# Attention outputs kept as features for the output projection, with maxima turned by VectorE, in a fp32 adaLN block on one Trainium2 core

## The chip, the cores and the metric

The kernel runs on one NeuronCore of a Trainium2 chip. A core has TensorE (PE: matmuls and transposes, with its weight loads as PEld), VectorE (DVE), ScalarE (ACT), GpSimd (POOL) and SyncE (SP), each with an instruction stream of its own, and 16 DMA engines, which are fed from queues; SP's and GpSimd's are used here. A matmul leaves its result in a PSUM bank; every bank holds 128 x 512 numbers of fp32, and in attention the scores, maxima, outputs and small transposes take their banks in turn.

The metric is the device time in microseconds (us), as a median over runs of the whole program.

## The reference

One transformer block with adaptive layer norm, on 2048 rows (S) of 576 features (D), with 32 heads of 18 features (DH) and 4608 hidden features (F):

```python
mod = (_silu(c) @ w_mod).reshape(c.shape[0], 6, 1, -1)
sa, ca, ga, sb, cb, gb = (mod[:, 0], ..., mod[:, 5])
h = _layernorm(x) * (1 + ca) + sa
q, k, v = heads of (h @ wqkv)                 # 32 heads, Dh = 18
p = softmax(q @ k.T * Dh ** -0.5)
x = x + ga * ((p @ v as (S, D)) @ wo)
h = _layernorm(x) * (1 + cb) + sb
x = x + gb * ((sigmoid(h @ w_gate) * (h @ w_up)) @ w_down)
```

All of it is fp32. The kernel gets there with pairs: a number is split into a part `hi` that the matmul format fp32r holds exactly, and the rest `lo`, and a product is made of hi x hi, hi x lo and lo x hi.

## The kernel before

**Stages.** The modulation, the first layer norm and the projections of q, k and v take 236 us; q and k go to DRAM (`qd`, `kd`) as features x rows, in two parts. Attention runs from 236 to 1597 us. The gated part with its products (L1028) and the way down (L1064) takes the rest, to 2927 us.

**Attention's units and steps.** Attention has 32 units. Unit u has a pair of heads, p = u mod 16, and one half of the queries (1024 of them; half 0 in units 0 to 15, half 1 in units 16 to 31). Each unit has 16 steps, kt = 0 to 15, one for 128 keys. What a step does stands in a string of letters, one for odd and one for even steps, which fixes PE's order by hand (the scheduler puts PE's instructions as they are written; it sorts those of the other engines itself):

- `t` is one score matmul (L927), keys x queries, followed by the exponential on ScalarE (L931). Four in a step.
- `v` is `values()`: the exponentials of two steps ago times the values (L548). The accumulator has four groups of 32 partitions, one for each head and half of the unit's queries: 18 features and, in row 18 (DH), the sum of the exponentials. All 16 steps add up in one bank.
- `m` is `turn()`, one step of the generator `maxima()` for a later unit: a matmul queries x keys (L446), of which VectorE takes the maximum over 512 keys (L452). In the units called paired, ScalarE puts one bank in four into SBUF (`over`, L455) and VectorE takes the maximum of that and of another bank in one instruction (L457). The table `SINGLE` names the units that aren't paired. The last of a unit's maxima comes seven steps before the unit starts, at kt 9 of the unit before it; the negated maxima `nm` (L464) have queries on partitions, 128 x 16.
- `k` is `taken()`: at kt 1 the finished accumulator of the unit before is copied by ScalarE into `oT` (L562), which has one buffer. ScalarE does its work in order: the exponentials behind the copy wait until `oT` is free.
- `w`, in odd steps, takes one step of whatever else is under way.

**What hangs on `w` before the change.** At kt 3 `outputs()` turns `oT` with four PE transposes (L572) so that queries lie on partitions, VectorE takes the reciprocals of the sums from PSUM (L576), ScalarE copies the bank back to `oT` (L587), and GpSimd multiplies by the reciprocals (L591) into `Oa` (half 0) or `big` (half 1), row layout. Eight steps of `m` after a unit's maxima are through, `spread()` turns `nm` with one PE transpose (L477), ScalarE and VectorE split it into two parts (L480, L481) and SP writes four rows (L485) into the unit's `q` tile: the score matmul gets the maximum as two more rows of its contraction. In steps 240 to 436 `w` also advances `first_rows()`: `load_wo()`, then `project_o(t)` for the row tiles t = 0 to 7 (output projection: transposes of `Oa`, L652 and L669, a split on VectorE and GpSimd, 28 matmuls L685, the residual), the second layer norm's statistics, and the tiles' transposition and splitting into operands, on GpSimd for the most part. From then on it advances `last_rows_project()`, tiles 8 to 15 over the first 384 features; the other 192 go through DRAM (`oend`) and are done by `last_rows()` amid the gated part, with transposes of its own (L1124, L1131).

**Loads.** `load_heads(u + 2)` stands at the start of unit u: eight SP transfers for the q tile (one of three) and the k tile (one of three) of the unit after next. In steps 64 to 239 GpSimd also prepares the weights of the way down (`down_parts`), with transfers on its own queue.

## Time and profile before

| | us |
|---|---|
| median of 3 runs | 2933.69 |
| the three runs | 2927.91, 2933.69, 2934.46 |
| profiled execution, its own time | 2929.86 |
| profiled execution, span | 2927.5 |

The granted clock of TensorE is 0.995 over the span. The span runs from the first to the last instruction; the execution's own time has a little around it.

How to read the rows in the prediction. The busy line names each engine, its busy time, its share of the span and its instructions. A row of single instructions has the start in us, the duration, the engine, the line of the kernel, the operation, the output and inputs with their shapes, and in brackets how long the engine had been idle and what ended that. A grouped row has the line, engine, operation, output<-inputs, shapes and count, then the busy time and the mean in ns of one, then the idle time in front of the group's instructions and what ended it. Rows with "x6: 616/617/618, 492.0 to 692.1" give a count, the smallest, median and largest duration in ns, and the start of the first and the last one.

### The profile page before, as it was taken

What the parts mean: (1) busy time and instruction counts of PE and PEld (TensorE: products, weight loads), DVE (VectorE), ACT (ScalarE), POOL (GpSimd) and SP (SyncE); (2) the same over time, 40 slices, a digit from 0 to 9 for tenths busy, and PEclk for the clock granted to TensorE, in tenths of its full rate; (3) what the DMA queues carried; (4) which work ended last, traced back from release to release, by engine and by line L of the source; (5) the groups of instructions that cost most, each with busy time, mean ns of one, the idle gap of its engine ahead of it and who ended that gap; (6) DMA issues with size and microseconds to landing.
All of it is one profiled execution on the core that took longest, in us unless ns stands there. A gap on an engine that the chain in (4) does not pass through costs nothing.

```text
span 2927.5 us, 46356 instructions
## 1 busy us (share of the span) xinstructions
PE 2848.3 (97%) x17141; PEld 1879.6 (64%) x17141; DVE 2218.6 (76%) x4023; ACT 1581.4 (54%) x2955; POOL 649.4 (22%) x829
## 2 busy tenths in 40 slices
PE   7999999999999999999999899999999999999998
PEld 6964333333444444444443788877888888888888
DVE  7277888888899988999982878789777555555555
ACT  3216889999987778998788333333332111111111
POOL 3122014544213110761102222233221100000000
PEclk9999999999999999999999999999999999999999
DMA  5344124333212110222125866677556844554443
GB/s 180 120 157 128 52 76 140 133 120 123 84 56 76 35 56 23 101 98 66 52 87 177 284 216 234 231 277 247 207 201 233 301 170 167 167 168 167 159 159 136
DMA packets 136745, 429.25 MB, mean 147 GB/s; under 512 B 18884, under 2 KB 56520, under 8 KB 124232
## 3 DMA queue, kind: packets, MB, share of 16 engines
q1 hardware_dynamic: 120472, 344.99, 35.0%
q0 software_dynamic: 16048, 81.31, 7.9%
q8 instruction: 135, 2.21, 0.3%
q14 instruction: 90, 0.74, 0.1%
HBM read 267.77 MB, written 157.95 MB: 145 GB/s over the span
## 4 chain that ended last, share of the span: by engine, by line
PE 82%; DVE 7%; ACT 4%; DMA 3%; issue 3%; SPq 1%; POOL 0%; POOLq 0%; ACTq 0%; DVEq 0%
PE o L548 16%; PE d L1064 14%; PE x L1028 12%; PE s L446 11%; PE s L927 10%; PE bu L1028 4%; PE bg L1028 4%; PE s L274 4%; ACT p L931 3%; PE s L325 2%; PE s L685 2%; DVE mx L452 1%; DVE w L1020 1%; DMA B<-hs 1%; PE s L572 1%
## 5 line engine op out<-in xcount | busy, mean ns | idle before, releaser
L452 DVE TENSOR_REDUCE mx<-s 128x1 f32<-128x512 f32 x1696 | 1076.6, 684 | 126.3 <-PE s L446 108.3
L931 ACT ACTIVATE p<-s 128x512 f32<-128x512 f32 x2048 | 1068.4, 610 | 146.7 <-PE s L446 75.2
L446 PE MATMUL s<-k,q 54*128 54x512 f32 x1920 | 608.4, 451 | 12.2 <-ACT p L931 6.6
L548 PE MATMUL o<-p,vaug 128*32 128x512 f32 x4096 | 554.8, 607 | 0.5 <-ACT p L931 0.4
L927 PE MATMUL s<-q,k 56*128 56x512 f32 x1920 | 552.6, 425 | 1.3 <-DMA q<-mrows 0.8
L1064 PE MATMUL d<-wd,hh 128*128 128x288 f32 x2304 | 468.3, 297 | 20.8 <-DVE Oa L1068 20.2
L927 PEld LDWEIGHTS s<-q,k 56*128 56x128 f32 x1920 | 260.5, 186 | 295.2 <-DVE mx L452 184.7
L446 PEld LDWEIGHTS s<-k,q 54*128 54x128 f32 x1920 | 273.6, 184 | 250.3 <-ACT p L931 172.3
L1064 PEld LDWEIGHTS d<-wd,hh 128*128 128x128 f32 x2304 | 373.4, 188 | 35.6 <-DVE Oa L1068 26.4
L1068 DVE TENSOR_TENSOR Oa<-Oa,d 128x288 f32<-128x288 f32 x576 | 256.0, 452 | 125.5 <-PE d L1064 120.3
L1064 PE MATMUL d<-wd,hl 128*128 128x288 f32 x1152 | 340.7, 296 | 0.0
L1028 PE MATMUL x<-k,w 128*128 128x512 f32 x1008 | 242.4, 390 | 4.7 <-DVE u L1239 2.4
L1040 ACT ACTIVATE u<-u 128x512 f32<-128x512 f32 x72 | 45.5, 632 | 318.3 <-DVE u L1228 312.1
L1064 PEld LDWEIGHTS d<-wd,hl 128*128 128x128 f32 x1152 | 216.9, 188 | 0.0
L1028 PEld LDWEIGHTS x<-k,w 128*128 128x128 f32 x1008 | 186.7, 188 | 42.5 <-DVE u L1239 3.5
L548 PEld LDWEIGHTS o<-p,vaug 128*32 128x32 f32 x4096 | 83.4, 108 | 163.9 <-issue 151.4
L1037 ACT ACTIVATE sg<-x 128x512 f32<-128x512 f32 x36 | 21.5, 599 | 304.3 <-PE x L1028 304.3
L1070 POOL DMA_DIRECT2D out_dram<-Oa x16 | 8.7, 543 | 606.0 <-DVE Oa L1068 606.0
L455 ACT ACTIVATE over<-s 128x512 f32<-128x512 f32 x176 | 105.1, 597 | 33.5 <-PE s L446 28.4
L1028 PE MATMUL x<-big,w 128*128 128x512 f32 x504 | 120.6, 390 | 1.0 <-issue 1.0
L1028 PE MATMUL x<-w,w 128*128 128x512 f32 x504 | 121.0, 390 | 0.0
L457 DVE CUSTOM_DVE_ANT_0 over<-s,over 128x512 f32<-128x512 f32 x176 | 120.2, 683 | 0.3
(232 smaller groups left out, 3605.1 us busy)
## 6 DMA issues: line engine op xcount, KB each, us to landing
ws<-w SPq DMA_DIRECT2D x126, 640.0 KB
w<-ws SPq DMA_DIRECT2D x126, 640.0 KB
wd<-wds SPq DMA_DIRECT2D x36, 1152.0 KB
k<-kd SPq DMA_DIRECT2D x60, 360.0 KB
wds<-w POOLq DMA_DIRECT2D x18, 1152.0 KB, 4.5
k<-kd SPq DMA_DIRECT2D x60, 180.0 KB
w<-in_B_w_down_dram POOLq DMA_DIRECT2D x18, 576.0 KB, 4.3
q<-qd SPq DMA_DIRECT2D x64, 144.0 KB
```

Source lines behind the costliest of these rows:

```text
L274: nc.tensor.matmul(acc, w, hT[:, t, cols], start=n == 0, stop=n == len(ts_) - 1)
L325: nc.tensor.matmul(acc[:, 0:HALF], hT[:, k, rows], w, start=n == 0, stop=n == len(ts_) - 1,)
L446: nc.tensor.matmul(sp, qs[rows, qt * P : (qt + 1) * P], ks[rows, at * 512 : (at + 1) * 512], start=True, stop=True,)
L452: nc.vector.tensor_reduce(to, sp, axis=AX.X, op=ALU.max)
L455: nc.scalar.activation(over, sp, AF.Relu)
L457: nc.vector.tensor_tensor_reduce(out=over, in0=sp, in1=over, scale=1.0, scalar=LOWEST, op0=ALU.add, op1=ALU.max, accum_out=mx[:, h * n + q ...
L548: nc.tensor.matmul(acc[32 * j : 32 * j + 32, :], vaug[:, kt, (2 * p + h) * VW : (2 * p + h) * VW + 32], probs[2 * c + h], start=kt == 0, s ...
L927: nc.tensor.matmul(sT, ks[rows, kcols], qs[rows, c * 512 : (c + 1) * 512], start=True, stop=True)
L931: state["exp"] = nc.scalar.activation(pr, sT, AF.Exp, scale=SCALE)
L1028: nc.tensor.matmul(acc[v], w[:, v, a, :], X[s][:, b, :], start=first and n == 0, stop=n == 6, skip_group_check=not first,)
L1064: nc.tensor.matmul(acc[:, :HALF], a[:, f, rows], w[:, f, cols], start=n == 0, stop=n == 5)
L1068: nc.vector.tensor_add(Oa[:, t, cols], Oa[:, t, cols], acc[:, :HALF])
```

## The change

**Outputs.** `taken()` now asks `outputs()` for a list of seven entries, one for each following `w`: at kt 1, right behind the copy, SP gathers the four rows of sums of `oT` into `sums`, 128 x 16; in the next `w` VectorE takes their reciprocals, SP writes these to DRAM and reads them back, each row spread over 32 partitions, into `full`, 128 x 512. Three `w` later GpSimd multiplies `oT` by `full`, and makes the two parts; two later SP stores both parts to the DRAM tile `od`, features x queries. No transposes by PE, no copy back on ScalarE. `full` and the parts lie in `Oa` (units of half 0), `big` (half 1) or a temporary (unit 30's outputs), in three places used in turn, and for the last unit in tiles of the exponentials.

**Maxima.** `nm` gets 128 x 32 with zeros behind the 16 columns. VectorE turns it in blocks of 32 x 32 (L466), makes the two parts (L468, L469) at once, and SP writes them to DRAM (`rows_m`) and reads four rows from there into the `q` tile. `spread()` is gone.

**Projection.** `project_o` reads its operands ready from `od`, one tile ahead, by SP; its transposes, copies and splits are gone, its matmuls stay. `last_rows()` reads the 192 features from `od` as well; its 16 transposes and the splits are gone, and so is `oend`. `last_rows` starts at n >= 11 instead of 5.

**Order.** The order by hand now holds for VectorE and SP too, and not for PE alone. `load_heads(u + 2)` stands behind step kt = 1 of unit u, and thus behind the gather. `SINGLE` has units 19 and 20 no more, so that they are paired. `FROM1` is eight steps later, and `load_wo` takes four more steps.

On SP, between unit 7 and unit 8, `q` being the tile of queries, `k` that of keys, and `mrows` the rows of maxima, this stood before:

```order
L485 DMA q_981<-mrows 1x8x128 x4
L411 DMA q_983<-qd 36x1x1024
L414 DMA q_983<-qd 18x1024
L415 DMA k_2181<-kd 36x1x2560
L419 DMA k_2181<-kd 18x2560
...
L485 DMA q_982<-mrows 1x8x128 x4
```

and this stands there now, `sums` and `rec` being the sums and reciprocals, `Oa` the place of `full` and of the parts:

```order
L571 DMA sums<-oT 128x1x16
L413 DMA q_983<-qd 36x1x1024
L416 DMA q_983<-qd 18x1024
L417 DMA k_2190<-kd 36x1x2560
L421 DMA k_2190<-kd 18x2560
...
L575 DMA rows_r<-rec 128x16
L576 DMA Oa<-rows_r 128x1x512
L470 DMA rows_m<-parts 128x64
L475 DMA q_985<-rows_m 1x32x32 x4
L592 DMA od<-Oa 18x2x512 x4
```

The four loads come twice in both, once for each head. Where SP had the heads' loads and the rows of maxima alone, it now has the gather ahead of the loads and the spread, the rows by way of DRAM and the stores behind them.

On VectorE, where a unit's maxima end, this is the order now (`mx` holds the maxima over 512 keys, `s` is a PSUM bank):

```order
L452 TENSOR_REDUCE mx_992<-s_6587 128x1
L464 TENSOR_REDUCE nm_994<-mx_992 128x16
L466 STREAM_TRANSPOSE turned<-nm_994 128x32
L468 CAST parts<-turned 128x32
L469 TENSOR_TENSOR parts<-turned,parts 128x32
L452 TENSOR_REDUCE mx_993<-s_6609 128x1
```

Before, only the reduction to `nm` stood there, and fifteen rows later the subtraction that took the rows from PE's bank. Where the outputs are scaled, some thirty rows on, VectorE has this now:

```order
L452 TENSOR_REDUCE mx_993<-s_6954 128x1
L574 RECIPROCAL rec<-sums 128x16
L457 ISA over,mx_993<-s_6960,over 128x512
L457 ISA mx_993 128x1
L452 TENSOR_REDUCE mx_993<-s_6963 128x1
```

The reciprocal stood among the reduces before too, but read PE's bank; it now reads `sums`, which SP's transfer writes.

The diff, cut to its core; of longer removed pieces only the first and the last line are shown, since the kernel before has them:

```diff
@@ -38,7 +38,7 @@
-FROM0, FROM1 = 15 * 16, 27 * 16 + 5
+FROM0, FROM1 = 15 * 16, 27 * 16 + 13
@@ -46,7 +46,7 @@
-SINGLE = (0, 1, 16, 17, 18, 19, 20, 27, 28, 29)
+SINGLE = (0, 1, 16, 17, 18, 27, 28, 29)
@@ -234,7 +234,9 @@
-    oend = dram.tile([P, 8, D - DL], F32, name="oend")
+    od = dram.tile([2, D, S], F32R, name="od")
+    rows_m = dram.tile([P, 2, 32], F32R, name="rows_m")
+    rows_r = dram.tile([4, 512], F32, name="rows_r")
@@ -420,11 +422,14 @@
     mxs = [small.tile([P, 2 * HW // P, 4], F32, name=f"mx{i}", bufs=1) for i in range(2)]
+    nms = [small.tile([P, 32], F32, name=f"nm{i}", bufs=1) for i in range(2)]
+    for nm in nms:
+        nc.gpsimd.memset(nm, 0.0)
     def maxima():
         n = HW // P
-        last = None
         for u in range(UNITS):
             qs, ks = heads(u)
             mx = mxs[u % 2]
@@ -460,32 +460,23 @@
                     )
                 if i < 8 * n - 1:
                     yield
-            nm = small.tile([P, 2, n], F32, name="nm")
-            nc.vector.tensor_reduce(
-                nm.rearrange("p h t -> p (h t)"), mx, axis=AX.X, op=ALU.max, negate=True
-            )
-            last = (qs, nm)
+            nm = nms[u % 2]
+            nc.vector.tensor_reduce(nm[:, 0 : 2 * n], mx, axis=AX.X, op=ALU.max, negate=True)
+            turned = small.tile([P, 32], F32, name="turned", bufs=1)
+            nc.vector.transpose(turned, nm)
+            parts = small.tile([P, 2, 32], F32R, name="parts", bufs=1)
+            nc.vector.tensor_copy(parts[:, 0, :], turned)
+            nc.vector.tensor_sub(parts[:, 1, :], turned, parts[:, 0, :].bitcast(F32))
+            nc.sync.dma_start(rows_m.bitcast(F32), parts.bitcast(F32))
+            by = rows_m.rearrange("(b c) l j -> l c b j", c=32)
+            for h in range(2):
+                for l in range(2):
+                    to = 64 * h + 3 * DH + l
+                    nc.sync.dma_start(
+                        qs[to : to + 1, :].rearrange("l (t b j) -> l t b j", b=4, j=32).bitcast(F32),
+                        by[l : l + 1, n * h : n * (h + 1)].bitcast(F32),
+                    )
             yield
-        for _ in range(8):
...
-                )
@@ -560,40 +551,50 @@
             half, p, acc = state.pop("whole")
             oT = epool.tile([P, 512], F32, name="oT")
             nc.scalar.copy(oT, acc)
-            state["end"] = (half, p, oT)
...
-            state["last"] = epool.tile([P, 512], F32, name="oT")[:, 0 : 16 * DH].rearrange("p (t e) -> p t e", t=8)
+            todo_out.extend(outputs(half, p, oT))
+    todo_out = []
+    def outputs(half, p, oT):
+        at = turns["out"] = (turns["out"] + 1) % 3
+        if state["room"] is None:
+            full, hi, lo = (ppool.tile([P, 512], F32, name=f"p{i}") for i in range(3))
+        else:
+            room = state["room"][:, 1536 * at : 1536 * (at + 1)]
+            full, hi, lo = (room[:, 512 * i : 512 * (i + 1)] for i in range(3))
+            parts = room[:, 512:1536]
+        sums, rec = (epool.tile([P, 16], F32, name=n) for n in ("sums", "rec"))
+        def gather():
+            nc.sync.dma_start(sums, oT[DH::32, :].rearrange("j (q e) -> j q e", e=16))
+        def spread():
+            nc.vector.reciprocal(rec, sums)
+            nc.sync.dma_start(rows_r.rearrange("j (q e) -> (j q) e", e=16), rec)
+            nc.sync.dma_start(full, rows_r.unsqueeze(1).to_broadcast([4, 32, 512]))
+        def scaled():
+            nc.gpsimd.tensor_mul(full, full, oT)
+            nc.gpsimd.tensor_copy(hi.bitcast(F32R), full)
+            nc.gpsimd.tensor_sub(lo.bitcast(F32R), full, hi)
+        def stored():
             for h in range(2):
-                nc.vector.tensor_tensor(
...
-            )
+                f0 = (2 * p + h) * DH
+                for c in range(2):
+                    q, q0 = 32 * (2 * h + c), half * HW + c * 512
+                    if state["room"] is None:
+                        for l, part in enumerate((hi, lo)):
+                            nc.sync.dma_start(od[l, f0 : f0 + DH, q0 : q0 + 512].bitcast(F32), part[q : q + DH])
+                        continue
+                    nc.sync.dma_start(
+                        od[:, f0 : f0 + DH, q0 : q0 + 512].rearrange("l f q -> f l q").bitcast(F32),
+                        parts[q : q + DH].rearrange("f (l q) -> f l q", l=2),
+                    )
+        return [gather, spread, None, None, scaled, None, stored]
@@ -632,62 +633,51 @@
                 load(t + 2)
             yield
         weights.extend((wo_h, wo_l, we))
-        for _ in range(4):
+        for _ in range(8):
             yield
-    def project_o(t):
...
-        src = Os[t // 8][:, t % 8, :]
+    def load_o(t):
+        T = temp([P, 2048], F32R)
         n = 4 if t < 8 else DL // P
-        oh = T[:, 0 : n * P]
...
-            nc.gpsimd.tensor_sub(ol, full, oh.bitcast(F32))
+        cols = slice(t * P, (t + 1) * P)
+        for l in range(2):
+            nc.sync.dma_start(
+                T[:, 512 * l : 512 * l + n * P].rearrange("p (i q) -> p i q", q=P).bitcast(F32),
+                od[l, 0 : n * P, cols].rearrange("(i p) q -> p i q", p=P).bitcast(F32),
+            )
+            if t < 8:
+                nc.sync.dma_start(T[64 * l : 64 * l + 64, 1024:1152].bitcast(F32), od[l, DM:D, cols].bitcast(F32))
+        xt = Oa[:, t, :] if t < 8 else raws.tile([P, 2, 3, 256], F32, name="raw1", bufs=2).rearrange("p v t c -> p (v t c)")[:, 0:D]
+        nc.sync.dma_start(xt, x_rows[:, t, :])
+        return T, xt
+    def project_o(t0, t1):
+        ahead = load_o(t0)
         yield
-        if t < 8:
...
-            nc.gpsimd.dma_start(x1p[:, t - 8, :], xt)
+        for t in range(t0, t1):
+            wo_h, wo_l, we = weights
+            T, xt = ahead
+            if t + 1 < t1:
+                ahead = load_o(t + 1)
...
+                nc.vector.tensor_add(xt[:, cols], xt[:, cols], acc[:, 0:HALF])
+                yield
+            if t >= 8:
+                nc.gpsimd.dma_start(x1p[:, t - 8, :], xt)
     def ln_rows(z, t, x1, eng):
@@ -754,8 +744,7 @@
-        for t in range(8):
-            yield from project_o(t)
+        yield from project_o(0, 8)
@@ -849,8 +838,7 @@
-        for t in range(8, NT):
-            yield from project_o(t)
+        yield from project_o(8, NT)
@@ -885,17 +873,18 @@
-    manual.enter_context(tc.manual_schedule(engines={mybir.EngineType.PE}))
+    manual.enter_context(tc.manual_schedule(engines={mybir.EngineType.PE, mybir.EngineType.DVE, mybir.EngineType.SP}))
...
-        if 0 < u < UNITS - 2:
-            load_heads(u + 2)
+        if u == UNITS - 1:
+            state["room"] = temp([P, 2048], F32)
+            turns["out"] = 2
         if u == H // 2:
-            Os.append(big.tile([P, 8, 640], F32, name="big"))
+            state["room"] = big.tile([P, 8, 640], F32, name="big").rearrange("p a b -> p (a b)")
@@ -909,10 +898,10 @@
                 elif does == "k":
                     taken()
                 elif does == "w":
-                    if kt == 3:
-                        outputs()
-                    if "spread" in state:
-                        spread(*state.pop("spread"))
+                    if todo_out:
+                        does_out = todo_out.pop(0)
+                        if does_out:
+                            does_out()
                     if FROM0 <= step < FROM1:
                         next(rows0, None)
                     if step >= FROM1:
@@ -930,6 +919,8 @@
                     pr = probs[2 * c + h] = ppool.tile([P, 512], F32, name=f"p{2 * c + h}")
                     state["exp"] = nc.scalar.activation(pr, sT, AF.Exp, scale=SCALE)
             pending.append((half, p, kt, probs))
+            if 0 < u < UNITS - 2 and kt == 1:
+                load_heads(u + 2)
@@ -955,8 +946,6 @@
-            if u == UNITS - 1 and kt == 3:
-                nc.sync.dma_start(oend[:, :, 0 : D - DL - 2 * DH], Os[1][:, :, DL : D - 2 * DH])
@@ -968,10 +957,12 @@
+    state["room"] = None
-    outputs()
+    for does_out in todo_out:
+        if does_out:
+            does_out()
-    nc.sync.dma_start(oend[:, :, D - DL - 2 * DH :], state["last"])
@@ -1115,25 +1106,13 @@
             w = pool.tile([P, 2, 2, D], F32R, name="w")
             nc.gpsimd.dma_start(w, wod)
             for t0 in (0, 4):
-                od = pool.tile([P, 4, 256], F32, name="od")
...
-                    nc.tensor.transpose(pt[:, j * P : (j + 1) * P], od[:, j, 0:P], ident)
                 oh = pool.tile([P, 512], F32R, name="oh")
                 ol = pool.tile([P, 512], F32R, name="ol")
-                nc.vector.tensor_copy(oh, pt)
-                nc.vector.tensor_sub(ol, pt, oh.bitcast(F32))
-                pt = psum()
-                for j in range(4):
-                    nc.tensor.transpose(pt[:, j * P : (j + 1) * P], od[:, j, P:256], ident)
                 om = pool.tile([P, 512], F32R, name="om")
-                omh = pool.tile([P, 512], F32R, name="omh")
-                nc.vector.tensor_copy(om[0:64], pt[0:64])
-                nc.vector.tensor_copy(omh[64:P], pt[64:P])
-                nc.vector.tensor_sub(om[64:P], pt[64:P], omh[64:P].bitcast(F32))
+                cols = slice(HW + t0 * P, HW + t0 * P + 512)
+                for l, part in enumerate((oh, ol)):
+                    nc.sync.dma_start(part.bitcast(F32), od[l, DL:DM, cols].bitcast(F32))
+                    nc.sync.dma_start(om[64 * l : 64 * l + 64].bitcast(F32), od[l, DM:D, cols].bitcast(F32))
                 yield
                 for j in range(4):
                     rows = slice(j * P, (j + 1) * P)
@@ -1238,7 +1217,7 @@
-        if n >= 5 and n % 2:
+        if n >= 11 and n % 2:
```

113 lines of the change are left out of this document (15 added, 98 removed).

## The prediction

> **What bounds the kernel now.** I read the page's busy times first, then the windows of 50 us, then the rows of single instructions in attention.
>
> ```profile
> PE 2848.3 (97%) x17141; PEld 1879.6 (64%) x17141; DVE 2218.6 (76%) x4023; ACT 1581.4 (54%) x2955; POOL 649.4 (22%) x829
> 500.00:550.00 50.00, 49.26 (x329) 20.08 (x331) 44.61 (x84) 47.58 (x94) 21.06 (x35) 1.00 0.37 129
> 1000.00:1050.00 50.00, 49.77 (x339) 24.30 (x336) 45.65 (x85) 35.42 (x70) 8.50 (x17) 1.00 0.15 44
> 1150.00:1200.00 50.00, 49.69 (x335) 20.85 (x335) 45.96 (x87) 45.75 (x91) 26.33 (x32) 1.00 0.19 64
> ```
>
> The columns of a window are PE, PEld, DVE, ACT, POOL, granted clock, DMA share and GB/s. Three engines are nearly full at 500 us (PE 49.3, ACT 47.6, DVE 44.6 of 50), so none alone is the bound: each waits for the next one's banks or scores. GpSimd has at least 23 us of 50 free in each of these. So I don't price an edit by one engine's busy time but by what it adds to the cadence. A paired unit has one `over` (L455) in every two steps, which makes a clock:
>
> ```profile
> 599.88 0.60 ACT L455 ACTIVATE over<-s 128x512 f32<-128x512 f32 x1 [0.16 <-PE s L446]
> 605.17 0.60 ACT L455 ACTIVATE over<-s 128x512 f32<-128x512 f32 x1 [0.47 <-PE s L446]
> 610.03 0.60 ACT L455 ACTIVATE over<-s 128x512 f32<-128x512 f32 x1 [0.15 <-PE s L446]
> 615.12 0.60 ACT L455 ACTIVATE over<-s 128x512 f32<-128x512 f32 x1
> 620.40 0.60 ACT L455 ACTIVATE over<-s 128x512 f32<-128x512 f32 x1
> L562 ACT COPY oT<-o x6: 616/617/618, 492.0 to 692.1; 128x512 f32<-128x512 f32 x6
> 603.97 0.24 ACT L480 CAST mrows<-s 16x128 fp32r<-16x128 f32 x1
> 619.20 0.62 ACT L587 COPY oT<-s 128x512 f32<-128x512 f32 x1
> ```
>
> The spacings are 5.29, 4.86, 5.09 and 5.28 us. The plain one is 4.86. The first holds the turning of the maxima (L477, L480), the last that of the outputs (L572, L587); the third holds the copy L562, which stays. A whole unit is (692.1 - 492.0)/5 = 40.0 us.
>
> **The change, part by part.** *Turnings in attention.* Gone per unit are these:
>
> ```profile
> L572 PE MATMUL s<-ident,oT 128*128 128x128 f32 x128 | 21.0, 287 | 0.8 <-ACT oT L562 0.8
> L587 ACT COPY oT<-s 128x512 f32<-128x512 f32 x31 | 19.2, 619 | 0.0
> L477 PE MATMUL s<-ident,nm 128*16 128x128 f32 x32 | 8.9, 277 | 0.0
> L480 ACT CAST mrows<-s 16x128 fp32r<-16x128 f32 x32 | 7.6, 239 | 0.0
> L481 DVE TENSOR_TENSOR mrows<-s,mrows 16x128 fp32r<-16x128 f32 x32 | 9.0, 280 | 17.9 <-ACT mrows L480 17.3
> ```
>
> The cadence says 5.28 - 4.86 = 0.42 for the outputs and 5.29 - 4.86 = 0.43 for the maxima, 0.85 us a unit; 31 units have both within attention: **-26.4 us**. Bounds: 0 if something takes their place, and the sum of the groups above on PE and ACT, 56.7 us, if nothing overlapped.
>
> *VectorE's new work.* Per unit a 32x32-block transpose, a cast and a subtraction on 128x32 come in, L481 goes, and the reciprocal now reads SBUF. No transpose on VectorE stands in the trace; the nearest rows are small ones:
>
> ```profile
> L457 DVE DVE_READ_ACCUMULATOR2_ANT mx<- 128x1 f32 x176 | 14.6, 83 | 0.0
> L464 DVE TENSOR_REDUCE nm<-mx 128x16 f32<-128x64 f32 x32 | 6.7, 210 | 0.1
> ```
>
> So each costs 0.08 to 0.21 us, I take 0.14, 0.42 a unit, against 0.28 + 17.3/32 = 0.82 us that L481 and the wait in front of it held. VectorE's idle 5.4 us of 50 covers it in paired units; in the eight others it comes out even. **0**, between -3 and +5. [...]
>
> *GpSimd's new work.* Multiply, cast and subtract on 128x512 for each unit, in place of two small products (L591). Like shapes:
>
> ```profile
> L728 POOL TENSOR_TENSOR t<-t,t 128x512 fp32r<-128x512 f32 x9 | 11.6, 1285 | 0.4
> L726 POOL CAST t<-t 128x512 fp32r<-128x512 f32 x14 | 8.5, 611 | 0.2
> ```
>
> 1.28 + 0.61 + 1.28 = 3.2 us a unit, 101 us in all. Nothing on PE reads the result for another unit; what hides it is GpSimd's idle time. Its tightest place is the 1150 us window (26.3 of 50 busy). Were the cover gone, the next unit's copy into `oT` (one buffer) would stand and all of ACT behind it; the margin is the rest of the unit, more than 10 us. **0**, up to +5.
>
> *SP's transfers.* Per unit: sums in, reciprocals out, reciprocals spread, four stores of features, the maxima out, four reads of them (before: four). All stand in the written order now. How long a store and the read that waits for it take:
>
> ```profile
> 393.97 0.51 SPq L145 DMA_DIRECT2D gates<-w  x2
> 395.40 0.36 SPq L146 DMA_DIRECT2D gb_b<-gates  x1
> 309.59 0.52 SPq L145 DMA_DIRECT2D gates<-w  x2
> 314.03 0.34 SPq L146 DMA_DIRECT2D ga_b<-gates  x1
> ```
>
> 1.4 us from one issue to the other, and 4.4 with 2.6 MB queued in front. The maxima thus reach `q` two such trips after step 9, at worst 9 to 11 us, and are read at the unit's end, seven steps of 2.4 us later: hidden. The heads' loads start some 5 us later than now and are first read in step 9 of that unit: hidden. **0**; what it costs otherwise is rival A.
>
> *Output projection, tiles 0 to 7.* Gone are five transposes a tile on PE, two copies on VectorE and all of GpSimd's splitting; the 28 matmuls stay.
>
> ```profile
> L562 ACT COPY oT<-o x2: 587/587/587, 852.5 to 894.3; 128x512 f32<-128x512 f32 x2
> L562 ACT COPY oT<-o x6: 587/617/619, 1134.4 to 1340.3; 128x512 f32<-128x512 f32 x6
> L652 PE MATMUL s<-ident,Oa 128*128 128x128 f32 x32 | 5.2, 286 | 0.0
> L669 PE MATMUL s<-ident,t 128*128 128x128 f32 x8 | 2.5, 306 | 0.0
> L658 DVE COPY t<-s 128x512 f32<-128x512 f32 (+1 forms) x12 | 7.6, 636 | 0.1
> L670 DVE COPY t<-s 128x128 f32<-128x128 f32 x8 | 2.2, 278 | 0.0
> ```
>
> The five units from 894.3 to 1134.4 take 240.1 us; five like the one before (41.8) would take 209, so the eight tiles cost some 31. PE's transposes are 7.7 us of that, VectorE's copies 2/3 of 7.6 and 2.2, together 7.3; they overlap in part: **-6**, between 0 and -15. Units 19 and 20 become paired, 40.0 in place of 41.8: **-2**, between 0 and -3.6.
>
> *Tiles 8 to 15, and the last rows.*
>
> ```profile
> L652 PE MATMUL s<-ident,big 128*128 128x128 f32 x24 | 4.3, 287 | 0.0
> L1124 PE MATMUL d<-ident,od x8: 270/272/301, 1635.5 to 1705.4; 128*128 128x128 f32 x8
> L1131 PE MATMUL d<-ident,od x8: 272/272/273, 1636.4 to 1705.8; 128*128 128x128 f32 x8
>   issue: 2.1, 1
>   DMA od<-oend: 1.7, 1
> ```
>
> For tiles 8 to 15 4.3 us of PE go, but more of their matmuls now fall into paired steps, where ACT has less to spare: **-2**, between +3 and -4.3. In the gated part 16 transposes of 0.27 us go, 4.4 us, with a wait of 1.7: **-3**, between 0 and -6.
>
> *End of attention.* Unit 31's outputs pass sums, reciprocal, spread, GpSimd and eight stores, where PE and VectorE did it at once; the weights' stores (L1022) queue behind them on SP. PE doesn't wait for these outputs, but a late store holds a weight buffer. **+2**, between -2 and +10.
>
> Sum: -26.4 - 6 - 2 - 2 - 3 + 2 = -37.4. The profiled execution's span is 2927.5, its own time 2929.86; 2929.86 - 37.4 = 2892.5. The median of the runs, 2933.69, lies 3.8 above it, so **2896 us**, 1.3% faster.
>
> **Rivals.** *A, slower: VectorE stands at the reciprocal.* Its order is now written, and L574 stands among the reduces of step 3 and waits for the gathered sums; behind it are the reduces that free PE's banks, so a late gather stops attention.
>
> ```profile
> 611.96 0.62 ACT L562 COPY oT<-o 128x512 f32<-128x512 f32 x1
> 618.45 0.24 DVE L576 RECIPROCAL rec<-s 128x16 f32<-128x16 f32 x1
> ```
>
> The reciprocal keeps its place, 618.45 - 612.58 = 5.9 us after the copy's end. It decides from there on; break-even is 5.9 + 37.4/31 = 7.1 us. A gather of 8 us would cost 31 x (8 - 5.9) = 65 us: 2896 + 65 = 2961 us. For it: 128 pieces of 64 bytes, the 4.4 us trip above, GpSimd's weight traffic in units 4 to 15. Against: the gather stands ahead of the heads' loads, and the quiet trip is 1.4.
>
> *B, a larger gain.* The projection's own stretch was held by VectorE (45.65 of 50) and, freed of copies, falls by the full 15; the gated part and tail give 6 more: 2881.
>
> *C, half the gain.* The coupled engines give back what the turnings took: the plain 4.86 was reached because the previous steps had filled the banks, and half of the 26 comes back as waits for PE or ACT; with the projection at -3: 2917.
>
> *D, nothing.* GpSimd's 3.2 us land late, SP then holds the next gather, and small stalls eat the rest: 2930.
>
> **How the numbers follow.** Forecast 0.48 (2886 to 2908), B 0.15, C 0.17, D 0.06, A 0.14. Downwards the range reaches past B by the lower ends that B doesn't hold (VectorE 3, units 19 and 20 1.6 more, tiles 8 to 15 2.3 more, the end of attention 4 more: 11), upwards over C and towards D by the end of attention's upper end (8 more, 2917 + 8): 2870 to 2925. A measurement of this kernel tells 0.2%, 6 us, from no change; so faster is the forecast with B and C, 0.80, same is D, 0.06, slower is A, 0.14.
>
> **What would show it.** In the changed profile the spacings of `over` in a paired unit should be 4.86 but for the one with the copy, and the unit 39.1 to 39.2 us. No wait of DVE for a transfer into `sums` should be over a few us in total; a sum of tens of us there is A. The five units from 16 to 20 should take about 228 us; 215 is B. The `oT` copy should never wait for GpSimd; that would be D. PE should wait for no transfer into `q`. I am wrong in size if the spacings stay above 5.0 without a named wait, which is C.

## The result, and the profile after

| | before | changed |
|---|---|---|
| median, us | 2934.07 (4 runs) | 2954.02 (4 runs, 2948.64 to 2957.67) |
| ratio to before | | 1.007, 95% interval 1.0047 to 1.0092 |
| span of the profiled execution, us | 2927.5 | 2950.6 |
| mean granted clock | 0.995 | 0.987 |
| last copy of `oT` starts, us | 1595.5 | 1607.1 |
| from there to the end, us | 1332.0 | 1343.5 |

The change made the kernel 20 us slower. Of the 23 us of the span, 11.6 are lost up to the last copy of `oT` and 11.5 behind it. The busy line of the changed kernel's page comes first:

```profile
PE 2848.5 (97%) x16901; PEld 1876.0 (64%) x16901; DVE 2215.6 (75%) x4047; ACT 1570.4 (53%) x2908; POOL 684.8 (23%) x793
```

PE has 240 matmuls less and is as long busy as before (2848.3), while its idle time, the span less the busy time, grew from 79.2 to 102.1 us. So two things have happened: PE stands still for 23 us more, and what the missing matmuls saved was eaten up, since the matmuls that stayed took longer. The granted clock, 0.987 in place of 0.995, says where to look for the second.

**The turnings.** The view of ScalarE's single instructions over unit 9 has the cadence that the prediction read: an `over` in every two steps of a paired unit, 4.86 us when nothing else happens.

```profile
608.88 0.62 ACT L553 COPY oT<-o 128x512 f32<-128x512 f32 x1
...
612.05 0.60 ACT L455 ACTIVATE over<-s 128x512 f32<-128x512 f32 x1
...
616.89 0.60 ACT L455 ACTIVATE over<-s 128x512 f32<-128x512 f32 x1
...
631.49 0.60 ACT L455 ACTIVATE over<-s 128x512 f32<-128x512 f32 x1 [0.15 <-PE s L446]
...
636.78 0.60 ACT L455 ACTIVATE over<-s 128x512 f32<-128x512 f32 x1 [0.58 <-PE s L446]
...
641.64 0.60 ACT L455 ACTIVATE over<-s 128x512 f32<-128x512 f32 x1 [0.16 <-PE s L446]
```

Behind the copy the step of the outputs is now 616.89 - 612.05 = 4.84 where 5.28 stood; the step in which the maxima were turned, the last but one of the unit, is plain too (kt 13 in the table below). The two gains are there. But a new long one has come, 636.78 - 631.49 = 5.29 us, in steps kt 10 and 11, right after the unit's maxima end. The timeline of VectorE at that place, in unit 7, shows it (columns: start, duration, engine, line, operation, tiles):

```profile
550.40 0.69 DVE L452 TENSOR_REDUCE mx<-s 128x1 f32<-128x512 f32 x1
551.12 0.22 DVE L464 TENSOR_REDUCE nm<-mx 128x16 f32<-128x64 f32 x1
551.38 0.21 DVE L466 STREAM_TRANSPOSE turned<-nm 128x32 f32<-128x32 f32 x1
551.62 0.59 DVE L468 CAST parts<-turned 128x32 fp32r<-128x32 f32 x1
552.24 0.34 DVE L469 TENSOR_TENSOR parts<-turned,parts 128x32 fp32r<-128x32 f32 x1
552.51 3.16 DVE L452 TENSOR_REDUCE mx<-s 128x1 f32<-128x512 f32 x5
```

From 551.09 to 552.51 no bank of PE's is reduced, 1.4 us where 0.2 stood before. And the cast has no fixed price. The rows by line, over all 32 units, give the smallest, median and largest duration in ns:

```profile
L468 DVE CAST parts<-turned x32: 171/183/1373, 201.8 to 1559.9; 128x32 fp32r<-128x32 f32 x32
...
L469 DVE TENSOR_TENSOR parts<-turned,parts x32: 183/194/1304, 202.5 to 1560.1; 128x32 fp32r<-128x32 f32 x32
```

Of the 32 casts, 14 have no instruction of GpSimd beside them and take 0.17 to 0.18 us; the 18 others take 0.18 to 1.37. Two of the four over 1 us lie beside the new multiplication of the outputs (L579). Steps kt 10 to 12 together are 25.4 us longer than before, and 14 us of that lie in units 15, 16, 22, 23 and 27, where the block from L464 to L469 took 2.2 to 2.5 us, against 0.9 to 1.7 in the others.

**Where each step went.** A step lasts from its first exponential to the next step's. The table sums the differences to the kernel before, in us, over units 1 to 31 by step (the projection's steps of units 15 to 20 have moved and mix into the columns), and over all steps by units; the last column is the stretch from the last copy of `oT` to the end.

| run | kt 3 | kt 7 | kt 10 to 12 | kt 13 | units 1-14 | 15-20 | 21-26 | 27-31 | last stretch |
|---|---|---|---|---|---|---|---|---|---|
| changed | -17.1 | +11.8 | +25.4 | -13.2 | -3.5 | +7.1 | +0.5 | +9.4 | 1343.5 |
| tiles 8 to 15 later | -15.4 | -0.9 | +24.8 | -12.9 | -2.5 | +7.7 | +1.3 | +3.0 | 1338.1 |
| turning set apart | -17.0 | +11.5 | +5.7 | -12.9 | -8.2 | -0.5 | -5.2 | +10.6 | 1340.4 |
| parts by reductions | -17.4 | +13.1 | -0.2 | -12.9 | -11.4 | -1.2 | -6.0 | +11.9 | 1340.5 |
| no stalls | -12.4 | -0.4 | -0.6 | -12.5 | -11.4 | -1.9 | -5.5 | -0.3 | 1329.3 |

**SP.** The 11.8 us at kt 7 are two places, in units 28 and 29. SP's own timeline in unit 28:

```profile
1434.97 0.49 SPq L421 DMA_DIRECT2D k<-kd  x1
1435.90 0.36 SPq L575 DMA_DIRECT2D rows_r<-rec  x1
1442.78 0.60 SPq L576 DMA_DIRECT2D big<-rows_r  x1
1443.47 1.02 SPq L645 DMA_DIRECT2D t<-od  x2
```

The reciprocals go out at 1435.9 and can be read back only at 1442.8, since the heads' 1.5 MB, 2 x (360 + 180 + 144 + 72) KB, stand in front of them in the DMA engines (run 10 tests this); SP stands there 6.5 us, and the tile for the projection (L645) is issued behind that. PE's view of waits has the us in all, the times and the longest:

```profile
PE d L1055 <- DVE Oa L1059: 25.7, 28, 4.5
...
PE s L676 <- DMA t<-od: 8.3, 3, 4.3
PE s L916 <- DVE mx L452: 8.0, 9, 1.4
```

and VectorE's, of the sums:

```profile
DVE rec L574 <- DMA sums<-oT: 22.2, 1, 22.2
```

PE's waits for the tiles are 4.35 us in unit 28 and 3.76 in unit 29, while the step got 7.3 and 6.0 us longer. The rest stands in the windows (us, then busy time of PE, PEld, DVE, ACT and POOL; third from the end the granted clock):

```profile
1444.00:1448.00 4.00, 2.54 (x20) 0.84 (x16) 3.42 (x6) 3.41 (x7) 0.00 (x0) 1.00 0.87 227
1448.00:1452.00 4.00, 1.12 (x4) 1.07 (x5) 0.00 (x0) 0.23 (x1) 1.47 (x2) 0.64 0.97 224
1452.00:1456.00 4.00, 4.00 (x19) 1.83 (x17) 2.22 (x4) 0.60 (x1) 1.68 (x2) 0.50 0.11 33
1456.00:1460.00 4.00, 4.00 (x31) 2.12 (x28) 3.30 (x6) 2.87 (x6) 0.00 (x0) 1.00 0.00 0
```

PE stood still from 1446.5 to 1450.9, and its clock was halved from 1449.1 to 1455.9, so it then worked 5.0 us at half clock. Half of that, 2.5 us, and the 4.35 come near the 7.3: these two stalls cost 1.6 to 1.7 times their own length. Between 280 us and the end of the products the kernel before has 3 stretches of half clock, 10 us together; the changed one has 14, 65 us. Half of the difference, 27 us, is the most that PE can have lost to the clock.

**The gated part** has the same pattern. The first wait above (L1055, the products waiting for VectorE's additions) is 25.7 us against 20.2 before, but its longest one 4.5 against 2.9. Before, the line was this:

```profile
PE d L1064 <- DVE Oa L1068: 20.2, 22, 2.9
```

And there is half clock behind the longest one now:

```profile
1940.00:1944.00 4.00, 0.40 (x3) 0.40 (x4) 3.97 (x8) 0.47 (x1) 3.07 (x3) 1.00 0.50 177
1944.00:1948.00 4.00, 4.00 (x20) 4.00 (x20) 3.54 (x7) 0.62 (x1) 0.60 (x1) 0.57 0.84 298
```

VectorE is full there (3.97 of 4), with the last rows' operands among the products' work.

### The profile page after: what moved, and what is told of

The parts are those of the page before. It is cut to its first block, busy times and chain, and to the rows that moved or that the text cites. A ratio compares the mean times of both kernels' runs of the same rounds, so it can differ in the third digit from the quotient of the medians.

```text
span 2950.6 us, 46231 instructions
## 1 busy us (share of the span) xinstructions
PE 2848.5 (97%) x16901; PEld 1876.0 (64%) x16901; DVE 2215.6 (75%) x4047; ACT 1570.4 (53%) x2908; POOL 684.8 (23%) x793
## 4 chain that ended last, share of the span: by engine, by line
PE 77%; DVE 11%; DMA 4%; issue 3%; ACT 3%; SPq 1%; POOL 1%; POOLq 0%; DVEq 0%; ACTq 0%
PE o L539 15%; PE d L1055 14%; PE x L1019 12%; PE s L446 10%; PE s L916 10%; PE bg L1019 4%; PE bu L1019 4%; DVE mx L452 4%; PE s L276 4%; PE s L327 2%; ACT p L920 2%; PE s L676 2%; DVE w L1011 1%; DMA xs<-ho 1%; DMA t<-od 1%
## 5 line engine op out<-in xcount | busy, mean ns | idle before, releaser
L452 DVE TENSOR_REDUCE mx<-s 128x1 f32<-128x512 f32 x1664 | 1057.3, 684 | 130.8 <-PE s L446 109.5
L916 PE MATMUL s<-q,k 56*128 56x512 f32 x1920 | 559.0, 429 | 11.6 <-DVE mx L452 8.0
L1055 PE MATMUL d<-wd,hh 128*128 128x288 f32 x2304 | 475.5, 301 | 27.9 <-DVE Oa L1059 25.7
L1055 PEld LDWEIGHTS d<-wd,hh 128*128 128x128 f32 x2304 | 378.4, 191 | 44.0 <-DVE Oa L1059 33.6
L1055 PE MATMUL d<-wd,hl 128*128 128x288 f32 x1152 | 343.8, 298 | 0.0
L1055 PEld LDWEIGHTS d<-wd,hl 128*128 128x128 f32 x1152 | 220.1, 191 | 0.0
L455 ACT ACTIVATE over<-s 128x512 f32<-128x512 f32 x192 | 114.6, 597 | 37.9 <-PE s L446 32.3
L457 DVE CUSTOM_DVE_ANT_0 over<-s,over 128x512 f32<-128x512 f32 x192 | 129.4, 674 | 0.0
```

Source lines behind the costliest of these rows:

```text
L452: nc.vector.tensor_reduce(to, sp, axis=AX.X, op=ALU.max)
L455: nc.scalar.activation(over, sp, AF.Relu)
L457: nc.vector.tensor_tensor_reduce(out=over, in0=sp, in1=over, scale=1.0, scalar=LOWEST, op0=ALU.add, op1=ALU.max, accum_out=mx[:, h * n + q ...
L916: nc.tensor.matmul(sT, ks[rows, kcols], qs[rows, c * 512 : (c + 1) * 512], start=True, stop=True)
L1055: nc.tensor.matmul(acc[:, :HALF], a[:, f, rows], w[:, f, cols], start=n == 0, stop=n == 5)
```

## The experiments

In the expectations T is a theory and R its rival, and what was measured is held against them. The kernel before was timed anew beside each group of runs, with medians from 2931.2 to 2934.1 us, so a difference between runs of two groups is good to some 3 us. The letter n numbers the products of the gated part.

**1. The maxima on PE again.**

```diff
-            nc.vector.transpose(turned, nm)  ... parts, rows_m
+            last = (qs, nm)                  # and spread() as before, in w
```

> The changed kernel, but with the maxima turned by PE and split from PSUM as before the change; the outputs stay as features. Theory T (VectorE's block): the four VectorE instructions at the end of a unit's maxima (0.9 to 2.5 us in one piece) keep the reduces away that free PE's banks, and cost 24 us over the units in steps kt 10 and 11, against 13 us that the turning took in kt 13. Then this run has no excess over the kernel before in kt 10 and 11, kt 13 is as before, and the time is 2954 - 24 + 13 = 2943 us. Rival R (the loss is all in loads and stalls elsewhere, the maxima's new way saves its 13 us): 2954 + 13 = 2967 us.

Measured: 3013.82 us. Kt 10 to 12 lost their excess (-2.8) and kt 13 is as before (+0.5), as T has it, but neither of the two times came. With SP's order by hand the rows of maxima stand behind the stores of the outputs, which wait for GpSimd, and PE waits for them at the start of the next unit:

```profile
PE s L929 <- DMA q<-mrows: 40.9, 10, 9.4
```

The place of the loss is confirmed, its price is not; and the early turning has a use that I hadn't seen: it gets the rows into SP's order ahead of those stores.

**2. Tiles 8 to 15 one w later.**

```diff
-FROM0, FROM1 = 15 * 16, 27 * 16 + 13
+FROM0, FROM1 = 15 * 16, 27 * 16 + 15
```

> The changed kernel with the projection of tiles 8 to 15 begun one w later (FROM1 two steps later), so that no load of a tile stands in kt 3 behind SP's wait for the reciprocals. Theory T (SP in order): PE's two waits of 4.35 and 3.76 us in units 28 and 29 at kt 7, each with a stretch of half clock behind it, go: 2954 - 7.3 - 6.0 = 2941 us. Rival R (the heads' transfers fill the DMA engines and the tile is late wherever its load stands): the waits stay above 2 us, moved by a step or two, 2950 us or more.

Measured: 2945.88 us, kt 7 back to -0.9: T. The gain is 8 us by the medians in place of 13; units 27 to 31 gain 6.4, since PE got a new wait in unit 30 (2.3 us, with half clock behind it). The last stretch, which this edit doesn't touch, differs by 5.4 us between the two profiled executions.

**3. The last rows at n >= 5.**

```diff
-        if n >= 11 and n % 2:
+        if n >= 5 and n % 2:
```

> The changed kernel with the last rows begun at n >= 5 as before the change. Theory T (the place of the last rows): the three PE gaps of 3.8 to 4.5 us between 1939 and 2055 us come from VectorE's operand work of the last rows falling on the weights' and products' work; at the old place they are below 3 us and without half clock, and the gated part takes back 8 to 9 us: 2945 us. Rival R (the gaps come from the loads that now go to od, or from the time by which all is shifted): 2954 us within 3.

Measured: 2953.98 us, last stretch 1342.8; gaps of 3.9 and 5.4 us stay. T fell as it was put: n >= 5 isn't the old place. The last rows now take two steps less, so their operand work came four n earlier than before the change. Run 6 tests the right n.

**4. VectorE's turning set apart.**

```diff
+                if i in (2, 4, 6) and turning:
+                    turning.pop(0)()        # transpose; cast; subtraction and transfers
```

> The changed kernel with VectorE's transpose, cast and subtraction of the maxima set apart, two m apart each, in place of one block. Theory T (the block): each is 0.2 us and hides in VectorE's idle time; the excess in kt 10 and 11 falls from 24 us to under 8 and the stretches of half clock in units 15, 16, 23 and 27 go: 2936 us. Rival R (VectorE's time itself, 0.6 us a unit, is missing wherever it stands): 0.6 x 31 = 18 us stay, 2948 us.

Measured: 2937.57 us (1.0023, 1.0014 to 1.0032): T. That is 16 us less than the changed kernel by the medians, 14 by the ratios to the kernel before. The table has kt 10 to 12 at +5.7 from +25.4.

**5. Three stalls out at once** (2 and 4, and a ninth empty step in `load_wo`).

```diff
-        for _ in range(8):
+        for _ in range(9):
```

> Three of the stalls taken out together: VectorE's turning set apart (as in the run before that did so alone, 2937.6 us), tiles 8 to 15 begun one w later (alone worth 8 us), and the tiles 0 to 7 begun one w later too (a ninth empty step behind the weights wo), so that ScalarE's two table loads for the second layer norm no longer stand right behind the copy of oT in unit 20. Theory T (the loss is the sum of stalls, each with its half clock behind it): 2937.6 - 8 - 4 = 2925 us, with no PE gap above 2 us left between 300 and 1580 us. Rival R (the stalls share a cause, or move on to the next place when one is taken out): 2932 us or more, with gaps of the same size elsewhere.

Measured: 2943.63 us, slower than 4 alone: R by the time. The trace names two new stalls. The ninth step put a tile's load behind SP's wait in unit 17 (PE waits 4.7 us for `od`), and it shifted GpSimd's operand work onto the maxima in unit 22, which the next run's timeline shows.

**6. The same, the last rows at n >= 9.**

```diff
-        if n >= 11 and n % 2:
+        if n >= 9 and n % 2:
```

> The same, with the last rows begun at n >= 9. They take two steps fewer than before the change, so at n >= 9 their operand work starts at the same n (29) as before the change. Theory T (what counts is where the operand work falls): PE's gaps between 1900 and 2070 us are as before the change, none above 3 us, and the stretch from the last copy of oT to the end is 1332 to 1336 us in place of 1338 to 1343: 5 us less than the run without it. Rival R (the place within a few n doesn't matter, as the run at n >= 5 had it): the same within 3 us.

Measured: 2937.51 us, 6 less than run 5; the last stretch 1334.5 against 1341.9; no gap above 3 us behind 1900: T. The timeline of its unit 22, VectorE and then GpSimd:

```profile
1201.70 1.25 DVE L454 TENSOR_REDUCE mx<-s 128x1 f32<-128x512 f32 x2
1202.86 4.63 DVE L485 CAST parts<-turned 128x32 fp32r<-128x32 f32 x1
1207.41 1.28 DVE L454 TENSOR_REDUCE mx<-s 128x1 f32<-128x512 f32 x2
1208.61 2.65 DVE L488 TENSOR_TENSOR parts<-turned,parts 128x32 fp32r<-128x32 f32 x1
```

```profile
1203.74 1.27 POOL L747 TENSOR_TENSOR t<-t 128x512 f32<-128x512 f32 x1
1204.96 1.26 POOL L738 TENSOR_TENSOR t<-t,t 128x512 fp32r<-128x512 f32 x1
1206.18 1.26 POOL L747 TENSOR_TENSOR t<-t 128x512 f32<-128x512 f32 x1
...
1209.92 1.28 POOL L599 TENSOR_TENSOR big<-big,oT 128x512 f32<-128x512 f32 x1
```

A cast of 32 numbers per partition, 0.18 us in this run's median, takes 4.63 us and ends at 1207.49, within 0.05 us of the third of these instructions of GpSimd's (1206.18 + 1.26); the two reductions behind it, which read PE's banks, take their usual 0.64 each beside GpSimd's next instructions. The subtraction is stretched again, and ends within 0.06 us of the outputs' new multiplication (L599, 1209.92 + 1.28). Why the cast was held through three of GpSimd's instructions in a row, no row tells.

**7. Cast and subtraction on GpSimd.**

```diff
-            nc.vector.tensor_copy(parts[:, 0, :], turned)
-            nc.vector.tensor_sub(parts[:, 1, :], turned, parts[:, 0, :].bitcast(F32))
+            nc.gpsimd.tensor_copy(parts[:, 0, :], turned)
+            nc.gpsimd.tensor_sub(parts[:, 1, :], turned, parts[:, 0, :].bitcast(F32))
```

> The changed kernel with the maxima's cast and subtraction on GpSimd; VectorE keeps the 32x32 transpose. Theory T (the block on VectorE): the block shrinks from 0.9 to 2.5 us to 0.43, and what GpSimd does at that time can no longer stretch it: kt 10 and 11 keep under 10 us of their 24, the half clocks in units 15, 16, 23 and 27 go, 2940 us. [...]

Measured: 2974.31 us. Kt 10 to 12 fell to -0.7, T for the block, but the rows now queue behind GpSimd's weights, and PE waits:

```profile
PE s L916 <- DMA q<-rows_m: 32.6, 9, 6.4
```

**8. Order by hand for PE alone.**

```diff
-tc.manual_schedule(engines={mybir.EngineType.PE, mybir.EngineType.DVE, mybir.EngineType.SP})
+tc.manual_schedule(engines={mybir.EngineType.PE})
```

> The changed kernel with the order by hand for PE alone, VectorE's and SP's left to the scheduler as before the change. Theory T (the block and the loads are late by what they are, not by the hand's order): kt 10 and 11 keep their 24 us within 6, units 28 and 29 their waits, 2954 us within 6. Rival R (the order by hand costs or saves): the scheduler moves VectorE's four instructions apart or SP's tile loads ahead, and 10 us or more go; or the sums' transfer falls behind the heads' loads and VectorE stands at the reciprocal, more than 2970 us.

Measured: 2951.62 us (2937.17 to 2955.47), T by the time alone. By the rows T fell: the waits in units 28 and 29 went (kt 7 -0.6) and kt 10 to 12 kept 14.0 of their 25.4 us, while VectorE stood at the reciprocal and PE at the rows of maxima instead, by the views of the reciprocal's line and of PE's waits:

```profile
  DMA sums<-oT: 30.7, 6
```

```profile
PE s L916 <- DMA q<-rows_m: 11.0, 2, 8.5
```

Of the six, 25.2 us are the last unit's, with nothing behind it; the other five (5.5 us) are rival A of the prediction on a small scale. The hand's order, with the gather ahead of the loads, keeps it out.

**9. The parts by reductions** (on run 4).

```diff
-            nc.vector.tensor_copy(parts[:, 0, :], turned)
-            nc.vector.tensor_sub(parts[:, 1, :], turned, parts[:, 0, :].bitcast(F32))
+            nc.vector.tensor_reduce(parts[:, 0, :], turned[:, 0, :].unsqueeze(2), axis=AX.X, op=ALU.max)
+            nc.vector.tensor_reduce(turned[:, 1, :], parts[:, 0, :].bitcast(F32).unsqueeze(2), ..., negate=True)
+            nc.vector.tensor_reduce(parts[:, 1, :], turned.rearrange("p l j -> p j l"), axis=AX.X, op=ALU.add)
```

> The run with VectorE's turning set apart (2937.6 us), with the two parts made by three reductions of 128x32 (over an axis of one, the negated first part, the sum of two) in place of a cast and a subtraction. In that run the cast took 0.18 us in the median and 1.10 at most, beside GpSimd's work; the reduction to nm, which reads SBUF too, was 0.22 in all units. Theory T (casts and subtractions from SBUF wait for GpSimd's instructions, reductions don't): none of the three takes over 0.3 us, kt 10 to 12 lose their 5.7 us down to 2, and the time is 2934 us. Rival R (whatever VectorE reads from SBUF is stretched beside GpSimd, or the reading of nm was luck): some take 1 us and more, 2938 us or above.

Measured: 2931.3 us (0.9999, 0.999 to 1.0009), level with before. The three reductions over all units:

```profile
L486 DVE TENSOR_REDUCE parts<-turned x32: 174/177/186, 203.4 to 1541.8; 128x32 fp32r<-128x32 f32 x32
...
L487 DVE TENSOR_REDUCE turned<-parts x32: 174/186/188, 204.1 to 1542.0; 128x32 f32<-128x32 f32 x32
...
L493 DVE TENSOR_REDUCE parts<-turned x32: 168/213/222, 204.8 to 1542.2; 128x32 fp32r<-128x64 f32 x32
```

None over 0.23 us, with GpSimd's instructions as they were: T. One instruction more, and 6 us less than run 4.

**10. The heads' loads behind kt 3** (on run 4).

```diff
-            if 0 < u < UNITS - 2 and kt == 1:
+            if 0 < u < UNITS - 2 and kt == 3:
```

> The run with VectorE's turning set apart (2937.6 us), with the heads' loads moved from kt 1 to the end of kt 3, behind the reciprocals' way through DRAM and behind the tile's load that stands in kt 3. Theory T (SP stands some 6.5 us at the reading of the reciprocals, since their store queues behind the heads' megabyte, and the tile's load stands behind it): SP's wait there falls below 4 us, PE's waits for od in units 28 and 29 go, 2937.6 - 13 = 2925 us. Rival R (the heads' loads now come too late for the maxima of the unit after next, or the tile's load is slow by itself): PE waits for q, k or od for more than 5 us in all, 2935 us or more.

Measured: 3048.38 us. Kt 7 fell to -0.9, but the keys came too late for the maxima: R, and far dearer than I had it.

```profile
PE s L448 <- DMA k<-kd: 80.3, 19, 7.6
```

The loads bear the two steps, some 5 us, by which the change moved them, but not two more; the gather fits ahead of them, the reciprocals' way does not. The run also shows what SP had waited for in unit 28. With the heads' loads behind the reciprocals, SP's waits to read these back fell from the first of these rows, of run 4, to the second:

```profile
SPq L596 <- DMA rows_r<-rec: 227.6, 32, 16.0
SPq L596 <- DMA rows_r<-rec: 53.5, 32, 6.6
```

**11 and 12. Five edits together** (4, 9, 10, n >= 9, the statistics of the second layer norm one w later), and then with them the tiles of `x1p`, to which the last rows add their products, loaded four at a time.

```diff
         yield from project_o(0, 8)
+        yield
```

```diff
-                    xt = pool.tile([P, D], F32, name="xt", bufs=2)
-                    nc.sync.dma_start(xt, x1p[:, t0 + j, :])
+                xts = [pool.tile([P, D], F32, name="xt", bufs=4) for _ in range(4)]
```

> Four things together: VectorE's turning set apart, its parts by reductions, the heads' loads at the end of kt 3, the last rows begun at n >= 9, and the second layer norm's statistics one w later, off ScalarE's copy of oT in unit 20. Theory T (the loss is the sum of separate stalls, and without them the turnings' gain shows): attention ends near 1580 us counted from its start as before (15 less than before), the gated part is within 4 us of before, 2916 us, faster than the kernel before by half a per cent. Rival R (another stall takes the place of each one removed): 2926 us or more.

> The same, and the last rows' tiles of x1p loaded four at a time ahead of the first product in place of one by one. Theory T (PE waits for VectorE's addition, which waits for this load, 2.2 us in two places near 1690 us with half a clock behind): 2 to 4 us less than without, the gap near 1690 us is gone. Rival R (the DMA engines are full there, and the loads are late in any order): the same within 2 us.

Measured: 3032.37 and 3029.41 us, both lost to the heads' loads as in run 10. Between them the last stretch falls from 1337.1 to 1329.8, so the loads ahead are worth 3 us by the medians and 7 by this stretch, which is of one execution each.

**13. No stalls:** 4 and 9 with the tiles of run 2, n >= 9, the statistics one w later and `x1p` ahead; the heads' loads where the change has them.

> The run with the turning set apart and its parts by reductions (2931.3 us), the heads' loads at their place, tiles 8 to 15 begun one w later, the statistics one w later, the last rows begun at n >= 9 with x1p four tiles at a time. Theory T (separate stalls): units 28 and 29 lose their 14 us at kt 7, unit 20 some 3 us, the gated part 8 to 10 us with 1330 to 1333 us from the last copy of oT; 2931.3 - 25 = 2906 us, and half that if the stalls move: 2918. Rival R (the stalls move on in full when the phase of the program shifts): 2926 us or more.

Measured: **2908.88 us**, 0.992 of before (0.9904 to 0.9937): T. It beats both kernels. Attention's last copy of `oT` stands at 1576.3, the last stretch is 1329.3, six stretches of half clock are left between 280 us and the products' end, 24 us in all. The loads of `x1p` ahead are no part of the change, and their 3 to 7 us are in this time. The statistics were moved for the sake of these rows of ScalarE in unit 20 of the changed kernel, where two table loads stood right behind the copy and PE waited 2.5 us:

```profile
1088.68 0.59 ACT L553 COPY oT<-o 128x512 f32<-128x512 f32 x1
1089.16 2.07 ACT L920 ACTIVATE p<-s 128x512 f32<-128x512 f32 x4
1091.25 1.28 ACT L169 ACT_TABLE_LOAD   x1
1092.55 0.21 ACT L169 ACTIVATE sd<-var 128x8 f32<-128x8 f32 x1
1092.78 1.28 ACT L920 ACT_TABLE_LOAD   x1
```

**14. Units 19 and 20 unpaired again.**

```diff
-SINGLE = (0, 1, 16, 17, 18, 27, 28, 29)
+SINGLE = (0, 1, 16, 17, 18, 19, 20, 27, 28, 29)
```

> The same with units 19 and 20 unpaired again. The prediction gave the pairing 2 us. Theory T: units 15 to 20 take 0 to 3.6 us longer than without, the time is 2 us above. Rival R (ScalarE has more to do beside the statistics' table loads, and the pairing costs): equal or up to 3 us below.

Measured: 2910.44 us (2909.56 to 2914.86), 1.6 above run 13, whose runs go from 2905.36 to 2916.23. By the steps, units 15 to 20 are 2.2 us shorter without the pairing. The two disagree, and the term is too small for these runs: open.

## Why the prediction was wrong

**The turnings, -26.4: right a unit.** With nothing else in the way (run 9) units 1 to 14 are 11.4 us shorter, 0.81 a unit of the 0.85 predicted, and the copies of `oT` in the paired ones stand 39.1 to 39.2 us apart, as the prediction put it. In the changed kernel itself only 3.5 us of the 11.4 are left. Rival C, that the engines give the gain back, is out. (Its 2917 doesn't follow from its own terms either: 2896 + 13 + 3 is 2912. The measured time lies outside the range with both.)

**VectorE's new work, 0 and at most +5: this step failed first.** It was 25 us. Three errors are in it. The price: transpose, cast and subtraction are 0.21 + 0.18 + 0.19 = 0.58 in the median, not 0.42. The cover: I set it against the idle 5.4 us of 50 in a window, but the four instructions stand in one block, and PE runs out of reduced banks meanwhile (its waits for L452 are 8.0 us, up to 1.4 at a time, and four of the five over 1 us have half clock behind them); run 4 set them apart and took 14 to 16 us back with the same instructions. And the neighbour: I took the durations from rows that read PE's banks or were reductions, for a cast and a subtraction that read SBUF; the cast took 0.17 to 1.37 us in the changed kernel, where the four over 1 us end 0.03 to 0.05 us behind an instruction of GpSimd's, and up to 4.63 us in run 6. Run 9 took another 6 us back by the form alone. GpSimd's new 3.2 us a unit was priced at 0 by its own idle time; what it can cost stands on VectorE, beside which its new multiplication was seen twice in the changed kernel (casts of 1.19 us). How much of the 25 us that is no run tells, since casts took longer beside GpSimd's older work too, 1.28 us beside that on the weights (L625) and 1.37 beside that on the tiles (L727).

**SP's transfers, 0: second.** Two trips were reckoned at 9 to 11 us; the reciprocals' one alone took 6.9 us in unit 28. (The row of 4.4 us that stood for a full queue had one transfer of 1152 KB ahead of its store and a second one ahead of the read, 2.3 MB and not 2.6.) Still PE waited neither for the rows of maxima nor for the heads' tiles. But I didn't name what is queued behind SP's own wait: a tile's load, in units 28 and 29, 13 us. Runs 2 and 13 took it away.

**The projection and the pairing, -8: half open.** The changed kernel has +7.1 in units 15 to 20; VectorE's block and the table loads explain that sign, for without them (run 13) it is -1.9. The turnings' own 5 us are in that, so nothing is left of the 8, though a wait of 1.4 us with half clock in unit 20 counts against it. By the prediction's own test, the five units from 16 to 20 should have taken 228 us; they took 243 in the changed kernel and 239 in run 13. Whether the transposes' time was off the path there or something else took it, no run tells.

**Tiles 8 to 15, -2:** units 27 to 31 come out at -0.3 in run 13, where the turnings alone would give -3 to -4; a wait of 2.25 us with half clock in unit 30 is in it, so the tiles gave nothing or little.

**The last rows -3 and the end of attention +2: wrong as a pair in the changed kernel (+11.5), near in run 13 (-2.7).** The 2.7 us fit the removed transposes, though no run shows these apart; what went wrong is that with two steps less the operand work slid against the products' work on VectorE, and the loads of `x1p` lost their cover. Runs 6 and 12 took each back.

**Rival A, slower by the reciprocal,** had the right sign with the wrong place: VectorE's only wait for the sums is that of the last unit, with nothing behind it.

**What all terms missed:** each wait was priced at its own length. In the changed kernel most of PE's gaps of 1.2 to 4.5 us have 3.4 or 6.8 us of half clock behind them, and the prediction had no term for that. Of the 58 us between 2896 and 2954 it can be 27 at most. Run 13 is 24 us faster than the kernel before, of the 37 predicted, with the loads of `x1p` ahead in it; most of what is missing are the 8 us of the projection and the pairing, and 3 us that units 15 to 20 got longer apart from the turnings.

## What to carry to other kernels

Price a moved instruction not by an engine's idle share but by the longest piece in which it keeps that engine from its next consumer, and look who else works at that moment: a short cast from SBUF beside GpSimd took up to 25 times its median (4.63 us against 0.18, run 6). Behind every new wait in an order by hand, list what stands behind it up to the first instruction that PE needs (here a tile's load behind SP's 6.5 us). When the matmuls get fewer and PE's busy time doesn't, look at the granted clock (0.987 here, 0.995 before) as well as at the waits.

## What the runs showed of the hardware

In the profiled executions of the two kernels the granted clock changes, between 1.0 and 0.5, on one grid of 3.41 us; a stretch of half clock lasts one or two of these (3.41 or 6.83 us), but for the one that runs into the end. Between 280 us and the end, the two have 12 windows of that grid at full clock in which PE was idle for 1.93 to 3.40 us, and each was followed by half clock. Of the windows at full clock with 1.83 us or less, seven were followed by half clock, with 0.75 to 1.79 us of idle time, and the others, also some with 1.6 to 1.8 us, by full clock; what decides there is open. So one gap of 1.16 us at 918 us of the changed kernel, with smaller ones in its window, was followed by half clock, and one of 2.9 us at 2029 us of the kernel before, across two windows, was not.

The other surprise is that a cast of 128x32 took 0.17 to 4.63 us in run 6 (L485), and a reduction of the same tile to the same place in run 9 (L486) 0.17 to 0.19 in all units. The changed kernel's reduction to `nm` (L464), which reads SBUF too, took 0.21 to 0.22 us in all 32 units, in 17 of them beside an instruction of GpSimd's.
